# A re-planned order, single-block VectorE rounds and a folded last layer, without zero-weight matmuls

## The chip, the cores and the metric

The kernel runs on one core of a Trainium2 chip. A core has TensorE (PE, matrix products into the accumulation memory PSUM), VectorE (DVE), ScalarE (ACT, activation functions and copies), GpSimd (POOL) and SyncE (SP, here the queue that issues every DMA). The metric is the device time of one execution in microseconds.

## The reference

The input x has 2,048 rows of 512 features. Four layers are applied in turn, A, B, A, B, each to a layer norm of x and each added to x.

```python
def _A_ref(x, wq, wk, wv, wo):          # H = 32 heads, Dh = 16, one shared k and v
    q = (x @ wq).reshape(B, S, H, Dh).transpose(0, 2, 1, 3)
    k = x @ wk; v = x @ wv
    scores = jnp.einsum("bhqd,bkd->bhqk", q, k) * (Dh ** -0.5)
    o = jnp.einsum("bhqk,bkd->bhqd", softmax(scores), v)
    return o.transpose(0, 2, 1, 3).reshape(B, S, H * Dh) @ wo

def _B_ref(x, wqkv, wo):
    q, k, v = split_heads(x @ wqkv)      # 32 heads of 16 each
    phi = lambda t: jnp.where(t > 0, t + 1, jnp.exp(t)) + 1e-6
    pq, pk = phi(q), phi(k)
    kv = jnp.einsum("bhsd,bhse->bhde", pk, v); z = pk.sum(s)
    o = jnp.einsum("bhsd,bhde->bhse", pq, kv) / (pq . z + 1e-6)
    return o.transpose(0, 2, 1, 3).reshape(B, S, D) @ wo

x = x + _A_ref(layernorm(x)); x = x + _B_ref(layernorm(x))
x = x + _A_ref(layernorm(x)); x = x + _B_ref(layernorm(x))
```

Layers 0 and 2 are softmax attention, layers 1 and 3 linear attention.

## The kernel before

x is kept on the chip as 16 tiles of 128 rows (`x_sb`). Everything is issued by a planner: the class `Planner` holds operations with durations (`dur`), latencies (`lat`), priorities (`prio`) and dependencies, runs them through an event queue as the program is built, and writes the order it arrives at as the fixed instruction stream of each engine (`_dispatch1` picks, `emit` writes, with one semaphore wait per producing engine). Nothing is scheduled on the chip itself; a duration that is wrong only makes the fixed order a poor one. PSUM has eight banks: six in two sets of three for score blocks, bank 6 (`ACC`) for the weighted values, bank 7 and what is left over for the rest.

Softmax attention (`run_a`). Queries of a tile lie in four row groups j with two parities, so a layer has 64 segments (`a_segs`) and 2,048 blocks of 128 keys by 512 query columns. TensorE makes scores with 32-row matmuls that lie side by side in the array (L807, three or four in a group), and sums weighted values with 32-column matmuls, four side by side (L861). A block goes one of two ways. `act_stream` gives two or three blocks to one ScalarE exp (L973, 1024 or 1536 wide). One further block may ride along in the same score group and go to VectorE: `dve_take` turns scores into bf16 bit patterns with one add and maximum (L1049), and after each four such blocks `dve_shifts` makes three shifted copies (L1080), whose four versions are summed with weighted values (`VW`). VectorE blocks start only with an exp's score group, when `dve_open` or `dve_split` finds the backlog small enough. ScalarE's stream is in strict order; two sets of banks allow one group of scores to be made while the other is read.

Linear attention (`run_b`). `tile_` makes k and v of a tile, `q_` its q, `phi` their positive map (ScalarE exp at L1205, two VectorE operations). `kv_` sums keys by values over groups of tiles, `den` and `main` form numerator and denominator, divide (L1364, L1420), transpose, project (L575) and add to x (L1448). A tile's work of one layer starts when the layer before has finished that tile, so much of layer 1 lies beside layer 0's attention and much of layer 3 beside layer 2's. Only the last tile's chain and what needs the whole key sum comes after: the handover at 735 to 760 us and the tail after 1508 us.

Zero-weight matmuls. When TensorE has nothing to do the planner lets two functions add work whose stationary operand is zero: `fill` (L906, in attention) and `fill_lin` (L793, elsewhere). `fill` looks at a running count of columns:

```python
n = int(min(512, pl.work(0), (min(nxt) - pl.now) * 2400 if nxt else 512)) // 64 * 64
```

They add zero to a sum or write a bank that is cleared afterwards.

Of the kernel before, what the change touches and what calls it, by code (L numbers as in the profile page):

```python
# [15 lines left out]
P = 128  # L16
# [19 lines left out]
class Planner:  # L36
# [3 lines left out]
    def __init__(self, nc):  # L40
        self.nc = nc
        self.now = 0.0
        self.events = []
        self.seq = 0
        self.ready = {e: [] for e in ENGS}
        self.busy = {e: False for e in ENGS}
        self.until = {e: 0.0 for e in ENGS}
        self.order = {e: [] for e in ENGS}
        self.writer = {}
        self.readers = {}  # L50
        self.flags = {}
        self.flagwait = {}
        self.level = (0.0, 0.0)
        self.due = []
        self.idle = []
        self.mode = None
        self.port = 0.0

# [63 lines left out]
    def _dispatch(self, e):  # L122
        self._dispatch1(e)
        if e == PE and not self.busy[e] and self.idle:
            self.due = [t for t in self.due if t > self.now]
            for f in self.idle:
                f()

    def _dispatch1(self, e):
# [4 lines left out]
        while h:  # L134
# [5 lines left out]
            if o.port and self.port > self.now:  # L140
                held.append(x)
                continue
            if e == PE and STICK and o.mode != "row" and o.mode != self.mode != "row":
# [10 lines left out]
            if e == PE:  # L154
                if self.mode != o.mode:
                    dur += SWITCH
                self.mode = o.mode
# [6 lines left out]
            if o.begun:  # L164
                self.at(self.now, o.begun)
            self.at(self.now + dur, lambda: self._freed(e, o))
# [4 lines left out]
        if held and not self.busy[e] and e != PE:  # L171
# [124 lines left out]
    def emit(self, e, eng):  # L296
        waited = {}
        for o in self.order[e]:
# [7 lines left out]
            for k, d in need.items():  # L306
# [9 lines left out]
class Seg:  # L316
# [11 lines left out]
    def take(self, js, back=False):  # L328
# [12 lines left out]
QK_DUR = 0.225  # L341
PV_DUR = 0.225
QK_LAT = 0.365
SWITCH = 0.105
DH_DUR = 0.22
AH_DUR = 0.28
MCRIT = {0: (), 1: (0, 1), 2: (), 3: ()}
# [11 lines left out]
BLS = 1.4  # L359
BLO = 3.0  # L360
BLT = 4.0
# [6 lines left out]
DENS = {1: [[0], [1], [2], [3], [4], [5], [6], [7], [8, 9], [10, 11], [12, 13], [14, 15]],  # L368
        3: [[0], [1, 2], [3, 4, 5], [6, 7, 8, 9], [10, 11, 12], [13, 14, 15]]}
# [3 lines left out]
RESA = {1: (), 3: ()}  # L373
# [18 lines left out]
def bass_interleave_layers__grouped_kv_mqa__linear_attn_block__prompt_kernel(  # L392
# [42 lines left out]
    eps1 = sb("eps1", [1, H], BF16)  # L435
    warm = sb("warm", [P, 1], FP32)
# [117 lines left out]
    pool_op(lambda e: e.memset(eps1[:], 1e-6), ["eps"], dur=0.1, prio=2.1)  # L554
    pool_op(lambda e: e.memset(mask8[:], 1.0), ["mask8"], dur=0.3, prio=2.3)
# [231 lines left out]
    lin = {"a": False, "next": -1.0}  # L787

    def fill_lin():
        if lin["a"] or pl.busy[PE] or ("x", 3, T - 1) in pl.flags:  # L790
            return
        n = 128
        op({PE: (n / 2300.0, lambda e: e.matmul(ps[0:32, ACC * 512:ACC * 512 + n], lhsT=V0[:], rhs=zz[:], start=True, stop=True))},  # L793
           reads=["zz"], writes=[B_(ACC)], prio=9.0, lat=0.13, mode="col").cols = n

    pl.idle.append(fill_lin)

    def run_a(L):
# [34 lines left out]
        def pv_try():  # L833
# [32 lines left out]
            o = op({PE: (PV_DUR, fn)}, reads=list({x[3] for x in items}) + [("V" if x[5] is None else "VW", x[0]) for x in items], writes=[B_(ACC)], prio=2.0, lat=0.13, mode="col")  # L866
# [15 lines left out]
        def retry():  # L882
            if state.get("next", -1.0) <= pl.now:
                state["next"] = pl.now + 0.1
                pl.at(state["next"], lambda: pl._dispatch(PE))

        def fill():
            if cur["i"] >= len(segs) or state["done"] or not state["on"]:
                return
            sg = segs[cur["i"]]  # L890
            js = [j for j in range(4) if 0 < sg.sent[j] < sg.need[j]]
            spare = [b for b in banks.free if not retire.get(b)] if not banks.wait else []
            nxt = [t for t in pl.due if t > pl.now]
            n = int(min(512, pl.work(0), (min(nxt) - pl.now) * 2400 if nxt else 512)) // 64 * 64
            clear = not sg.submitted and all(o.done for o in pl.ws(B_(ACC)) + pl.readers.get(B_(ACC), []))
            if n >= 128 and not js and not clear and not spare:
                retry()
            if n < 128 or not (js or clear or spare):
                return
            if clear:  # L900
                b, j, st = ACC, 0, True
            elif js:
                b, j, st = ACC, js[-1], False
            else:
                b, j, st = spare[0], 0, True
            o = op({PE: (n / 2400.0, lambda e: e.matmul(ps[32 * j:32 * j + 32, b * 512:b * 512 + n], lhsT=V0[:],  # L906
                                                       rhs=QT[:, sg.t, 0:n], start=st, stop=st))},
                   reads=[("QT", sg.t)], writes=[B_(b)], prio=9.0, lat=0.13, mode="col")
            o.cols = n

        pl.idle.append(fill)

        def act_stream():
# [4 lines left out]
            state["on"] = lin["a"] = True  # L918
            while True:
# [50 lines left out]
                if chunk["blk"] and stale():  # L970
                    dve_close()
                p_ = yield ("acq", pt_pool, 0.0)
                ex = op({AC: (0.05 + 0.4267 * n, lambda e, n=n, s_=s_, p_=p_: e.activation(PT[:, p_, 0:n * 512], ps[:, s_ * 512:(s_ + n) * 512], ACTF.Exp, scale=EXPSC, bias=EXPBIAS))},  # L973
                        writes=bk + [("PT", p_)], prio=1.0, lat=0.17)
                ex.begun = lambda n=n: pl.due.append(pl.now + 0.05 + 0.4267 * n + 0.17)
                pl.give_after(sets, s_, [ex] if split is None else [ex, p1])
                pv_post(ex, [(sg, kt, j, PT[:, p_, i * 512:(i + 1) * 512], ("PT", p_)) for i, (sg, kt, j) in enumerate(group)], [n, [], pt_pool, p_])
            state["done"] = True
            pv_kick()
# [64 lines left out]
        def dve_take(extra, own):  # L1044
# [4 lines left out]
            o = op({DV: (0.60, lambda e: e.tensor_scalar(out=dst.bitcast(I16), in0=bank(b), scalar1=VB, scalar2=VLO, op0=ALU.add, op1=ALU.max))},  # L1049
# [7 lines left out]
            return o  # L1057

# [7 lines left out]
        def dve_shifts(blk, f_, hold):  # L1066
# [3 lines left out]
            for w in range(1, NSH):  # L1070
# [8 lines left out]
                en, du = (PO, n / 1165.0 + 0.25) if pool else (DV, n / 3840.0 + 0.066)  # L1079
# [117 lines left out]
    ph_pool = Pool_(range(NPH))  # L1197

    def run_b(L):
# [3 lines left out]
        def phi(b, dst, key, pr, n=D, join=None, after=()):  # L1203
            i = yield ("acq", ph_pool, pr)
            op({AC: (0.07 + n / 1200.0, lambda e: e.activation(phE[:, i, 0:n], bank(b, n), ACTF.Exp))}, reads=[B_(b)], writes=[("phE", i)], prio=min(pr, 0.9))  # L1205
# [22 lines left out]
        def crit_v(t, sl, pr):  # L1228
# [5 lines left out]
            for h in range(2):  # L1234
                src, dst = bank(bs[h], 256).rearrange("p (h d) -> p h d", d=DH), va_v[:, sl, 16 * h:16 * h + 16, 0:DH]
                c = op({AC: (AH_DUR, lambda e, dst=dst, src=src: e.copy(dst, src))}, writes=[B_(bs[h]), ("va", sl)], prio=pr, join=l)
# [4 lines left out]
        def tile_(t):  # L1241
# [19 lines left out]
            src, dst = bank(b).rearrange("p (h d) -> p h d", d=DH), va_v[:, sl, :, 0:DH]  # L1261
            if t >= CRIT:
# [7 lines left out]
        def q_(t):  # L1270
            pr = base(t) + 0.01 * t + 0.2
            yield ("flag", ("xnT", L, t))
            yield from until(("xnT", t))
            b = yield ("acq", banks, pr)
            mm4(bank(b), lambda g, k: wqkv[:, k, g * P:(g + 1) * P], lambda k: xnT[:, k, t * P:(t + 1) * P], [("xnT", t), "wqkv"], b, pr)
            yield from phi(b, QT[:, t, :], ("QT", t), pr)
            pl.flag(("bq", L, t))

# [175 lines left out]
        for t in range(T):  # L1454
            pl.process(tile_(t))
            pl.process(q_(t))
            pl.process(main(t))
        for ts in DENS[L]:
            pl.process(den(ts))
        for gi, ts in enumerate(KVG):  # L1460
            pl.process(kv_(gi, ts))
# [50 lines left out]
```

## Time and profile before

| | |
|---|---|
| median of 3 runs | 1555.51 us (1555.47 to 1560.37) |
| profiled execution, its own time | 1556.79 us |
| its span | 1555.1 us |
| PE, DVE, ACT busy share | 94%, 93%, 95% |
| first and last attention exp | 13.6 and 1508.0 us, with none from 736.2 to 759.5 |
| zero-weight matmuls, busy | 131.0 us (L906), 16.1 us (L793) |

A group's line gives source line, engine, operation, written and read tensors, shapes and count; then busy time and mean duration of one; then idle time of the engine ahead of them and what ended it. Matmul durations include the way through the array, so side-by-side matmuls overlap and a busy PE need not be at its peak. PEclk is the clock granted to TensorE, as a share of full speed.

### The profile page before, as it was taken

What the parts mean: (1) busy time and instruction counts of PE and PEld (TensorE: products, weight loads), DVE (VectorE), ACT (ScalarE), POOL (GpSimd) and SP (SyncE); (2) the same over time, 40 slices, a digit from 0 to 9 for tenths busy, and PEclk for the clock granted to TensorE, in tenths of its full rate; (3) what the DMA queues carried; (4) which work ended last, traced back from release to release, by engine and by line L of the source; (5) the groups of instructions that cost most, each with busy time, mean ns of one, the idle gap of its engine ahead of it and who ended that gap; (6) DMA issues with size and microseconds to landing.
All of it is one profiled execution on the core that took longest, in us unless ns stands there. A gap on an engine that the chain in (4) does not pass through costs nothing.

```text
span 1555.1 us, 36056 instructions
## 1 busy us (share of the span) xinstructions
PE 1458.7 (94%) x14602; PEld 535.4 (34%) x14713; DVE 1448.3 (93%) x2707; ACT 1476.8 (95%) x1500; POOL 68.8 (4%) x122
## 2 busy tenths in 40 slices
PE   8998999999999999999999989999999999999999
PEld 4322332333333333333644323323333333333345
DVE  7999999999999999998676799999999999999977
ACT  8999999999999999999699999899999999999982
POOL 4000000000000000000111000000000000000000
PEclk9999999999999999999999999999999999999998
DMA  5100010000000000000000000000000000000001
GB/s 132 47 2 1 8 22 5 8 8 5 8 8 8 5 8 5 1 1 1 2 1 1 1 1 15 15 8 8 6 9 5 8 8 8 5 5 2 1 2 55
DMA packets 40435, 17.55 MB, mean 11 GB/s; under 512 B 34128, under 2 KB 39760, under 8 KB 40272
## 3 DMA queue, kind: packets, MB, share of 16 engines
q1 hardware_dynamic: 40272, 15.25, 4.2%
q8 instruction: 118, 1.93, 0.5%
q14 instruction: 45, 0.37, 0.1%
HBM read 5.28 MB, written 2.10 MB: 5 GB/s over the span
## 4 chain that ended last, share of the span: by engine, by line
PE 32%; issue 23%; DVE 23%; ACT 20%; POOL 1%; DMA 0%; SPq 0%; ACTq 0%; POOLq 0%; DVEq 0%
ACT PT L973 19%; DVE FB L1049 11%; PE ps L861 11%; PE ps L807 9%; DVE FB L1080 6%; PE ps L575 4%; PE ps L906 2%; PE ps L732 2%; PE ps L1122 1%; POOL rs L655 1%; DVE st L651 1%; DVE sacc L1103 1%; PE ps L793 1%; ACT phE L1205 1%; DVE xn L658 1%
## 5 line engine op out<-in xcount | busy, mean ns | idle before, releaser
L973 ACT ACTIVATE PT<-ps 128x1024 bf16<-128x1024 f32 (+1 forms) x1361 | 1424.5, 1180 | 19.9 <-PE ps L861 13.4
L1049 DVE TENSOR_SCALAR FB<-ps 128x512 int16<-128x512 f32 x1017 | 675.0, 686 | 23.5 <-PE ps L807 20.7
L807 PE MATMUL ps<-QT,KM 32*128 32x512 bf16 x4096 | 533.4, 384 | 46.8 <-ACT PT L973 27.9
L861 PE MATMUL ps<-FB,VW 128*32 128x512 bf16 x4068 | 530.4, 385 | 19.5 <-ACT PT L973 9.5
L861 PE MATMUL ps<-PT,V 128*32 128x512 bf16 x3079 | 513.0, 386 | 9.7 <-ACT PT L973 5.6
L1080 DVE TENSOR_SCALAR FB<-FB 128x2048 int16<-128x2048 int16 (+1 forms) x765 | 503.0, 683 | 0.9
L807 PEld LDWEIGHTS ps<-QT,KM 32*128 32x128 bf16 x4096 | 139.8, 91 | 445.3 <-ACT PT L973 203.8
L861 PEld LDWEIGHTS ps<-FB,VW 128*32 128x32 bf16 x4068 | 133.4, 94 | 219.5 <-issue 113.0
L861 PEld LDWEIGHTS ps<-PT,V 128*32 128x32 bf16 x3079 | 125.9, 94 | 111.8 <-issue 56.1
L906 PE MATMUL ps<-QT,V 128*32 128x512 bf16 (+6 forms) x568 | 131.0, 315 | 0.9 <-DVE FB L1049 0.9
L655 POOL TENSOR_TENSOR rs<-ve,mhalf 128x1 f32<-128x1 f32 x64 | 51.7, 811 | 1398.9 <-DVE ve L653 1386.0
L575 PE MATMUL ps<-wqkv,xnT 128*128 128x512 bf16 (+1 forms) x211 | 65.1, 368 | 3.9 <-issue 2.9
L906 PEld LDWEIGHTS ps<-QT,V 128*32 128x32 bf16 x568 | 44.1, 95 | 59.6 <-issue 39.3
L1103 DVE COPY sacc<-ps 128x512 f32<-128x512 f32 x64 | 43.8, 684 | 7.8 <-PE ps L861 7.6
L1205 ACT ACTIVATE phE<-ps 128x512 bf16<-128x512 f32 (+1 forms) x66 | 41.3, 625 | 6.6 <-PE ps L732 4.7
L1122 PE MATMUL ps<-identF,sacc 128*128 128x128 f32 x256 | 45.9, 291 | 1.5 <-DVE sacc L1103 0.8
L732 PE MATMUL ps<-xnT,wqkv 128*128 128x128 bf16 x512 | 44.3, 221 | 0.0
L651 DVE BATCH_NORM_STATS2 st<-x_sb 128x6 f32<-128x512 bf16 x60 | 40.8, 683 | 2.6 <-DMA x_sb<-in_A_x_dram 2.3
L1105 DVE TENSOR_TENSOR sacc<-sacc,ps 128x512 f32<-128x512 f32 x56 | 38.2, 682 | 2.4 <-PE ps L861 2.1
L732 PE MATMUL ps<-xnT,wq 128*128 128x128 bf16 x480 | 38.6, 224 | 0.0
L575 PEld LDWEIGHTS ps<-wqkv,xnT 128*128 128x128 bf16 x272 | 21.8, 97 | 44.9 <-issue 34.2
L732 PEld LDWEIGHTS ps<-xnT,wqkv 128*128 128x128 bf16 x512 | 29.1, 98 | 22.8 <-issue 19.4
(115 smaller groups left out, 671.1 us busy)
## 6 DMA issues: line engine op xcount, KB each, us to landing
out_dram<-x_sb SPq DMA_DIRECT2D x16, 128.0 KB, 1.7
x_sb<-in_A_x_dram SPq DMA_DIRECT2D x3, 512.0 KB, 6.1
wqkv<-in_B_wqkv_dram SPq DMA_DIRECT2D x1, 1536.0 KB, 7.5
xnT<-xn SPq DMA_TRANSPOSE x36, 2.4
x_sb<-in_A_x_dram SPq DMA_DIRECT2D x4, 128.0 KB, 2.2
wq<-in_A_wq_dram SPq DMA_DIRECT2D x1, 512.0 KB, 4.2
wo<-in_A_wo_dram SPq DMA_DIRECT2D x1, 512.0 KB, 4.1
wo<-in_B_wo_dram SPq DMA_DIRECT2D x1, 512.0 KB, 8.5
```

What stands on the lines that cost most here:

```text
L575: return e.matmul(dst, lhsT=l, rhs=r, start=(k == 0), stop=(k == len(pairs) - 1))
L655: op({PO: (0.55, lambda e: e.tensor_tensor(out=rs[:, t:t + 1], in0=ve[:, t:t + 1], in1=mhalf[:], op=ALU.pow))}, reads=[("ve", t), "mhalf"] ...
L732: ins = e.matmul(dst[:, g * P:(g + 1) * P], lhsT=lhs(g, k), rhs=rhs(k), start=(k == 0), stop=(k == FT - 1))
L807: return e.matmul(bank(b), lhsT=KM[r, sg.par, kt * P:(kt + 1) * P], rhs=QT[r, sg.t, :], start=True, stop=True)
L861: ins = e.matmul(ps[32 * j:32 * j + 32, ACC * 512:(ACC + 1) * 512], lhsT=V[:, kt, :] if w is None else VW[:, kt, w, :], rhs=ap, start=(k = ...
L906: o = op({PE: (n / 2400.0, lambda e: e.matmul(ps[32 * j:32 * j + 32, b * 512:b * 512 + n], lhsT=V0[:], rhs=QT[:, sg.t, 0:n], start=st, sto ...
L973: ex = op({AC: (0.05 + 0.4267 * n, lambda e, n=n, s_=s_, p_=p_: e.activation(PT[:, p_, 0:n * 512], ps[:, s_ * 512:(s_ + n) * 512], ACTF.Ex ...
L1049: o = op({DV: (0.60, lambda e: e.tensor_scalar(out=dst.bitcast(I16), in0=bank(b), scalar1=VB, scalar2=VLO, op0=ALU.add, op1=ALU.max))}, wr ...
L1080: o = op({en: (du, lambda e, w=w, g_=g_: e.tensor_scalar(out=FB[:, g_, 0:n].bitcast(I16), in0=FB[:, f_, 0:n].bitcast(I16), scalar1=float(w ...
L1103: o = op({DV: (0.6, lambda e, src=src: e.tensor_copy(src, bank(ACC)))}, writes=[B_(ACC), key], prio=0.0, lat=0.15)
L1122: o = op({PE: (0.12, lambda e, c=c: e.transpose(ps[:, b * 512 + c * P:b * 512 + (c + 1) * P], src[:, c * P:(c + 1) * P], identF[:]))}, rea ...
L1205: op({AC: (0.07 + n / 1200.0, lambda e: e.activation(phE[:, i, 0:n], bank(b, n), ACTF.Exp))}, reads=[B_(b)], writes=[("phE", i)], prio=min ...
```

## The change

- `fill` and `fill_lin` are gone; what they read stays in memory, unused.
- `alone`: when VectorE's ready list is empty or its backlog under `DXB`, a single score matmul is issued for one VectorE block, in a free bank, without an exp.
- Planner: `soon` holds back a VectorE or ScalarE operation outside attention when a more urgent one will be ready before it would end; TensorE's cost of changing its mode is reduced by idle time; waits of one instruction are written in the order in which they are expected to end. Durations, latencies and backlog limits are set anew.
- Layer 1: q of tiles 4 to 13 starts after the last exp of layer 0 (`QLATE`); at most three q are under way.
- Layer 3 is folded. Keys by values are summed transposed (`kvt`) and multiplied with the output weights once (`mix`, giving 512 by 512). Per tile, `den3` forms every feature's denominator with four matmuls against a block-diagonal z, takes its reciprocal on ScalarE as exp(-ln(d + 1e-6)), and multiplies q with it on VectorE (tiles 4, 7 and 10 on GpSimd); `main3` is then four matmuls and the add to x (tiles 3, 7 and 11 add x on TensorE and copy on ScalarE).

```diff
-        pl.idle.append(fill)
...
+        def alone():
+            if state["done"] or not USE_DVE or ("K", L, KGATE) not in pl.flags or not banks.free or banks.wait or pl.backlog(DV) > DXB:
+                return
+            hit = dve_hit(set())
+            if hit is None:
+                return
+            x = hit + (banks.free.pop(0),)
+            qo = op({PE: (QK_DUR, lambda e: qk_mm(e, x[3], x[0], x[1], x[2]))}, reads=qk_reads(x[0], [x[1]]), writes=[B_(x[3])], prio=0.1, lat=QK_LAT - QK_DUR, mode="row")
+            qo.cols = 128
+            dve_take(x, True)
...
-QK_DUR = 0.225
-PV_DUR = 0.225
-QK_LAT = 0.365
-SWITCH = 0.105
+QK_DUR = 0.22
+PV_DUR = 0.222
+QK_LAT = 0.438
+SWITCH = 0.107
+ROWIN = 0.07
+PV_LAT = 0.215
+EX_LAT = 0.21
...
+QLATE = {1: range(4, 14), 3: ()}
...
-BLS = 1.4
-BLO = 3.0
-BLT = 4.0
+BLS = 1.2
+BLO = 5.0
+DXB = 2.0
+BLT = 3.0
...
         def q_(t):
...
+            if t in QLATE[L]:
+                yield ("flag", ("exps", L - 1))
...
+        def mix(g):
+            pr = 1.45 + 0.001 * g
+            b = yield ("acq", banks, pr)
+            mm(bank(b), [(kvT[:, g, :], wo2[:, g, :])], ["kvT", "wo2"], b, pr, 0.216)
...
+        def den3(t):
...
+            op({PE: (0.23, fn)}, reads=[("QT", t), "Zbd"], writes=[B_(b)], prio=pr, lat=0.2).cols = 512
+            af = [("FB", f_, i % 2 * 2), ("FB", f_, i % 2 * 2 + 1)]
+            o = op({AC: (0.5, lambda e: e.activation(rd, bank(b), ACTF.Ln, bias=epsc[:]))}, reads=["epsc"], writes=[B_(b), ("rd", i)], prio=pr, after=af)
+            pl.give_after(banks, b, [o])
+            op({AC: (0.5, lambda e: e.activation(rd, rd, ACTF.Exp, scale=-1.0))}, writes=[("rd", i)], prio=pr)
+            qn = FB[:, 1 + t // 4, t % 4 * 512:t % 4 * 512 + 512]
+            o = op({(PO if t in PQ else DV): (PQD if t in PQ else 0.6, lambda e: e.tensor_tensor(out=qn, in0=rd, in1=QT[:, t, :], op=ALU.mult))}, reads=[("rd", i), ("QT", t)],
+                   writes=[("qn", t)], prio=pr, after=[("FB", 1 + t // 4, t % 4)])
...
+        def main3(t):
...
+                mm(bank(b), pairs, keys, b, pr, 0.86 + SW[L] / 2)
+                o = op({DV: (0.6, lambda e: e.tensor_tensor(out=x_sb[:, t, :], in0=x_sb[:, t, :], in1=bank(b), op=ALU.add))},
+                       writes=[B_(b), ("x", t)], prio=pr)
```

## The prediction

> **What bounds the kernel now.** I read the page first, then the groups of instructions with their shapes kept apart, then busy time by stretch, then the timeline of TensorE. The page's slices come first:
>
> ```profile
> span 1555.1 us, 36056 instructions
> PE   8998999999999999999999989999999999999999
> DVE  7999999999999999998676799999999999999977
> ACT  8999999999999999999699999899999999999982
> PEclk9999999999999999999999999999999999999998
> ```
>
> Three engines are near full in the two attention layers, ScalarE most evenly. The stretches show who has room, and where:
>
> ```profile
> 13.00:720.00 707.00, 666.20 (x6663) 226.28 (x6710) 690.33 (x1265) 700.55 (x701) 28.28 (x40) 1.00 0.05 12
> 735.00:760.00 25.00, 23.86 (x304) 18.36 (x302) 14.04 (x46) 9.83 (x25) 2.05 (x4) 1.00 0.01 1
> 760.00:885.00 125.00, 117.80 (x1168) 51.38 (x1177) 89.10 (x193) 123.91 (x114) 13.57 (x29) 1.00 0.01 1
> 885.00:1500.00 615.00, 578.13 (x5744) 195.50 (x5789) 598.49 (x1080) 602.56 (x605) 16.34 (x15) 1.00 0.04 7
> 1508.00:1519.00 11.00, 11.00 (x138) 9.05 (x136) 6.67 (x21) 3.96 (x10) 0.55 (x1) 1.00 0.01 1
> 1519.00:1555.00 36.00, 32.45 (x289) 20.39 (x291) 27.00 (x46) 7.34 (x13) 0.00 (x0) 0.86 0.18 59
> ```
>
> The columns are length, then busy time of PE, PE loads, DVE, ACT and POOL, then the clock. ScalarE is idle 6.5 us of 707, 1.1 of 125 and 12.4 of 615: it sets the pace of attention. It rests 15.2 us in the handover at 735 to 760, and in the tail after 1519 it does only 7.3 us of 36. VectorE has 36 us of room at 760 to 885. Now the groups that the change touches:
>
> ```profile
> L973 ACT ACTIVATE PT<-ps 128x1024 bf16<-128x1024 f32 x1004 | 972.9, 1067 | 16.2 <-PE ps L861 11.8 <-PE ps L807 3.3
> L973 ACT ACTIVATE PT<-ps 128x1536 bf16<-128x1536 f32 x357 | 511.3, 1497 | 3.7 <-PE ps L807 1.8 <-PE ps L861 1.6
> L1205 ACT ACTIVATE phE<-ps 128x512 bf16<-128x512 f32 x62 | 39.7, 641 | 4.8 <-PE ps L732 4.7
> L562 ACT ACT_TABLE_LOAD x1 | 1.3, 1283 | 0.8 <-PEq L1497 0.8
> L906 PE MATMUL ps<-QT,V 128*32 128x512 bf16 (+6 forms) x568 | 131.0, 315 | 0.9 <-DVE FB L1049 0.9
> L793 PE MATMUL ps<-zz,V 128*32 128x128 bf16 x198 | 16.1, 228 | 0.0
> ```
>
> The last two are the zero-weight matmuls; nothing waits for them. Back-to-back ScalarE instructions overlap: start to start in the trace most exps are 0.904 us apart (1024 wide) and 1.331 us (1536), and the 512-wide ones 0.477.
>
> What the zero-weight matmuls may do shows in the clock, which leaves 1.0 at two places, 24.02 to 27.43 us and 1522.47 to 1532.7:
>
> ```profile
> 20.61:24.02 3.41, 3.01 (x42) 1.58 (x39) 3.41 (x13) 3.41 (x4) 1.99 (x5) 1.00 0.39 79
> 24.02:27.43 3.41, 3.08 (x16) 1.10 (x16) 2.48 (x10) 3.21 (x4) 1.78 (x4) 0.50 0.28 46
> 573.57:576.98 3.41, 2.33 (x22) 0.79 (x23) 3.41 (x7) 3.41 (x5) 0.00 (x0) 1.00 0.02 5
> 1519.06:1522.47 3.41, 3.41 (x60) 2.81 (x58) 3.36 (x8) 0.60 (x1) 0.00 (x0) 1.00 0.00 0
> ```
>
> PE's busy time does not tell these stretches apart; the columns streamed do. Four 512-column matmuls side by side show 0.40 us and eight 0.61, so a group takes 0.21. In multiples of that, matmuls streamed 44% of 20.61 to 24.02 and 19% of 1519.06 to 1522.47, and the clock halved after each; 43% of 573.57 to 576.98 did not halve it. The border is near 44%.
>
> **The change part by part.** The sum is made against the profiled execution's 1556.8 us (span 1555.1); the median of the runs is 1555.5, 1.3 below.
>
> *Exps.* In the built order of the new program ScalarE has 947 exps of 1024, 387 of 1536 and one of 512. At the distances above: -57 x 0.904 + 30 x 1.331 + 0.48 = -11.1 us. A few more copies of 0.47 us fall to ScalarE: +2.
>
> *Late q.* Ten tiles of the first linear layer compute q only after the first attention's last exp. Their ScalarE exps, 10 x 0.477 = 4.8 us, leave the full stretch and can lie in the 15.2 idle us of the handover: -5. Their 16 matmuls (1.07 us a tile) stand on TensorE behind the handover's own chain, which is hidden as long as that chain has the pauses that 7.4 us of zero-weight matmuls fill today. Tiles 4 to 13 of the second attention wait for these q; it begins with tiles 0 to 3.
>
> *Other waits.* Durations and sorted waits are re-planned. Bounds: 0, and all 19.9 us of idle before the exps. The VectorE rounds issued alone answer only part of what those rows name, so I take a third: -6. Attention together: -20, with ends -9 and -34 (-11 + 2, alone or with -5 and -20).
>
> *VectorE rounds.* 1,040 evictions instead of 1,017 and 783 shifts instead of 765, 0.60 us start to start: 24.7 us more. The cover is the 36 us at 760 to 885 and 8 us that late q frees (10 x 0.80); without it up to 24.7 would come back. Zero.
>
> *TensorE.* 147 us of zero-weight matmuls go. The program now holds 3,505 groups of score and value matmuls instead of 3,422, 70 of them a lone score matmul: 83 x 0.22 = 18 us more, in the freed time. POOL gets three multiplies in the tail (128x128 took 0.415 us, so an estimate of 1.7 each) beside 2.4 us per tile on ScalarE. SyncE's queue has the same transposes and stores in almost the same order: zero.
>
> *The clock in attention.* Counted again without the zero-weight columns, 28 of some 420 stretches of 3.41 us fall below 44%, against 1 with them. Laying the new order's matmuls beside its exps at the distances above I count about 20 (24 for the old order by the same method, so it counts a little low). The price of one: below, 0.3 us, what ScalarE lost in and after 24.02 to 27.43 (0.20 + 0.12), where no VectorE round hung on TensorE; above, half the stretch, 1.7. Attention asks TensorE for some 65% of its columns, so a halved stretch leaves about a quarter undone; between the ends I take 0.7: +14, with ends 0 (no fall) and 34.
>
> The row at 20.61 has only 0.40 us of idle PE and still precedes a fall. The Trainium skill, "TensorE: Matmul & The Clock Gate", section "HAM oscillation", puts the danger at idle gaps of TensorE above some 3.4 us; by that rule nothing in attention would fall, and the sum would lose the 14.
>
> *The clock in the tail's chain.* In 1512.23 to 1515.65 the real columns are 35% without L793, whose 37 matmuls run there for 2.2 us while the chain waits. The next matmuls (16 in 1.91 us) would run at half: +3, ends 0 and 6.
>
> *The folded last layer.* Now the tail needs 36.4 us from the last kv matmul to the end. New, per tile: four small matmuls, Ln and Exp on ScalarE, one multiply, four matmuls, one add. The built order has Ln and Exp in groups of two tiles with an activation table load ahead of each group, 18 loads. A pair of tiles: 2 x 1.283 + 2 x (0.48 + 0.64) = 4.81 us. VectorE needs 2 x 2 x 0.60 = 2.4 for it and TensorE about 2.1 (8 x 0.22 + 8 x 0.05), so ScalarE sets the tail. From there: masked z 0.7, first scores 0.4, Ln 0.6, load and Exp 1.8, two copies 1.0, seven pairs 33.7, a lone tile 3.8, three copies 1.4, then multiply, matmuls, add and 2.4 us of store: 5.3. That is 48.7 instead of 36.4; with a half-clocked end 0.7 more: +13. Ends: +10 (all at the short distance), and +36 if every load costs twice its row, since the one load seen had an idle engine before it. Should loads cost nothing here, -10.
>
> The load's row has no drain beside it. The Trainium skill, "ScalarE: Activation LUTs", section "What ACT_TABLE_LOAD costs", gives about 2.66 us for a switch, a drain of 1.38 included; 18 x 1.38 would add an estimated 25 us, 1591 in all.
>
> **Sum.** 1556.8 - 20 + 14 + 3 + 13 = 1566.8; against the median 1565.5, so 1566.
>
> **The rivals.**
> 1. *The clock holds* (faster). Place: attention and the tail's chain. For it: 573.57 stayed at 1.0 with 43%, and two falls are all the evidence for a border. Against: the fall at 24.02 with 44%. Both clock terms vanish: 1556.8 - 20 + 13 - 1.3 = 1548.5. It decides when the two clock terms together are under 2.3 us, some three cold stretches. The Trainium skill's rule, named under the clock in attention, would make this the outcome.
> 2. *Cold stretches at full price*: 20 x 1.7 = 34 instead of 14: 1586. For it: nearly all idle before the exps (15.1 of 16.2 us of the 1024-wide ones) already waits for TensorE. Against: the small loss at 24.02.
> 3. *A switch costs twice the load*: +23: 1589. For it: the only load row is before any work. Against: the activation after it followed at once. The Trainium skill's figure, named above, points here.
> 4. *The loads cost nothing* (the fold does what it can): -23: 1543. Against: the 1.283 us row. The Trainium skill, "ScalarE: Activation LUTs", section "Table sets", names a set that holds both functions; the built order loads between them all the same.
>
> **How the numbers follow.** Chances: forecast 0.40 (own range 1555 to 1577), rival 1 0.28, rival 2 0.15, rival 3 0.12, rival 4 0.05. Runs of this kernel tell 0.3% (4.7 us) from no change. Faster: three quarters of rival 1, rival 4 and a sliver of the forecast: 0.27; same: the rest of rival 1 and the forecast's low edge: 0.09; slower 0.64. Range 1541 to 1595: it cuts off about 0.07 below (rival 4 and the best of 1) and 0.10 above.
>
> **What would show it.** Right: clock rows of 0.50 scattered through 60 to 1490; exps ending about 6 us earlier than 1508 net; ScalarE above 90% busy in the tail with 18 loads of 1.28; a tail near 49 us. Wrong: a clock of 1.00 throughout attention, loads with idle time behind them, or a last exp after 1515.

## The result and the profile after

The changed kernel takes 1605.38 us (median of 4 executions, 1603.94 to 1606.78) against 1557.94 us of the kernel before beside it (1555.47 to 1561.19): 1.0313 times as long, interval 1.0297 to 1.0329. The direction was forecast, the size was not: 1605 lies beyond the range's upper end of 1595. The profiled execution took 1606.78 us, its span is 1604.9.

Lines of the page of the changed kernel, the same ones as shown of the kernel before:

```profile
span 1604.9 us, 34443 instructions
PE   7998998988888989888999888999988988899965
DVE  7999999999999999997776999999999999999943
ACT  7999999999999999997899998999999999999967
PEclk9989999999998998899999999999999999998977
```

The clock row has dips all along, and TensorE shows tenths of 8 where it had 9. At the right end VectorE and TensorE run down while ScalarE goes on. The stretches of the changed kernel (length, then busy time of PE, PE loads, DVE, ACT and POOL, the clock, DMA share and GB/s) are cut at its own first and last exps:

```profile
15.00:730.00 715.00, 638.53 (x6276) 206.95 (x6324) 688.45 (x1256) 696.20 (x672) 25.58 (x40) 0.96 0.05 12
745.00:773.50 28.50, 27.23 (x345) 21.62 (x345) 21.07 (x64) 13.28 (x34) 2.56 (x5) 0.94 0.01 2
773.50:900.00 126.50, 115.32 (x1142) 51.31 (x1150) 92.45 (x200) 120.80 (x115) 13.39 (x29) 0.95 0.01 1
900.00:1500.00 600.00, 535.28 (x5345) 175.48 (x5392) 583.94 (x1051) 582.38 (x578) 11.92 (x14) 0.97 0.03 7
1534.68:1550.00 15.32, 10.86 (x82) 6.47 (x76) 5.72 (x16) 3.35 (x9) 0.55 (x1) 0.80 0.00 1
1550.00:1604.90 54.90, 30.57 (x132) 13.00 (x135) 20.04 (x31) 45.38 (x56) 3.46 (x3) 0.72 0.12 39
```

ScalarE's idle time in the three attention stretches is now 18.8, 5.7 and 17.6 us, and the clock is 0.95 to 0.97 there. The groups say what ScalarE waits for:

```profile
L965 ACT ACTIVATE PT<-ps 128x1024 bf16<-128x1024 f32 x947 | 921.0, 1048 | 23.5 <-PE ps L828 15.2 <-PE ps L882 5.2 <-PE ps L762 0.2
L965 ACT ACTIVATE PT<-ps 128x1536 bf16<-128x1536 f32 x387 | 550.9, 1471 | 16.2 <-PE ps L828 11.2 <-PE ps L882 3.4
L1384 ACT ACT_TABLE_LOAD x9 | 11.5, 1283 | 0.2
L1386 ACT ACT_TABLE_LOAD x9 | 11.5, 1283 | 0.2
L1384 ACT ACTIVATE FB<-ps,epsc 128x512 f32<-128x512 f32 x16 | 10.2, 684 | 0.1
L1386 ACT ACTIVATE FB<-FB 128x512 f32<-128x512 f32 x16 | 9.3, 622 | 0.1
```

Idle before the exps was 19.9 us (16.2 + 3.7), two thirds of it for value matmuls; it is 39.7 now, 26.4 of it for score matmuls (L828). A wait that moves to the matmuls straight ahead of the exp is what a slower TensorE looks like. A fall is one or more stretches of 3.41 us in a row at 0.50. Within the span there are 25 falls, 140 us in all, against two falls and 13.7 us before. Here is one, the stretch ahead of it first:

```profile
489.61:493.02 3.41, 1.83 (x19) 0.59 (x19) 3.26 (x8) 3.41 (x4) 0.86 (x1) 1.00 0.03 7
493.00:496.41 3.41, 3.41 (x20) 0.62 (x17) 2.85 (x5) 2.86 (x4) 0.00 (x0) 0.50 0.16 33
```

In the first, matmuls streamed in 31% of the time; in the second TensorE is busy throughout at half speed and ScalarE stands still for 0.55 of 3.41 us.

Where the 49.9 us of span went, from the last attention exp's end (1507.98 us before, 1534.68 after): 26.7 us up to it, 23.2 behind it in what is called the tail below (47.1 us before, 70.3 after).

### The profile page after: what moved, and what is told of

It reads as the page before. It is cut to its first block, busy times and chain, and to the rows that moved or that the text cites. A ratio compares the mean times of both kernels' runs of the same rounds, so it can differ in the third digit from the quotient of the medians.

```text
span 1604.9 us, 34443 instructions
## 1 busy us (share of the span) xinstructions
PE 1407.3 (88%) x13836; PEld 495.2 (31%) x13943; DVE 1462.4 (91%) x2728; ACT 1516.9 (95%) x1521; POOL 66.2 (4%) x126
## 4 chain that ended last, share of the span: by engine, by line
PE 35%; DVE 31%; ACT 27%; issue 6%; DMA 0%; SPq 0%; POOL 0%; ACTq 0%; DVEq 0%; POOLq 0%
ACT PT L965 24%; PE ps L882 15%; DVE FB L1044 14%; PE ps L828 11%; DVE FB L1086 9%; PE ps L605 3%; PE ps L762 2%; PE ps L1128 2%; DVE sacc L1111 1%; DVE sacc L1109 1%; ACT phE L1213 1%; DVE st L681 1%; ACT L1386 1%; ACT L1384 1%; ACT FB L1384 1%
## 5 line engine op out<-in xcount | busy, mean ns | idle before, releaser
L965 ACT ACTIVATE PT<-ps 128x1024 bf16<-128x1024 f32 (+1 forms) x1335 | 1421.7, 1170 | 39.6 <-PE ps L828 26.4
L1044 DVE TENSOR_SCALAR FB<-ps 128x512 int16<-128x512 f32 x1040 | 687.0, 684 | 32.2 <-PE ps L828 28.6
L828 PE MATMUL ps<-QT,KM 32*128 32x512 bf16 x4096 | 550.0, 394 | 72.5 <-ACT PT L965 41.8
L882 PE MATMUL ps<-FB,VW 128*32 128x512 bf16 x4160 | 562.0, 397 | 39.6 <-ACT PT L965 27.8
L882 PE MATMUL ps<-PT,V 128*32 128x512 bf16 x3056 | 528.9, 396 | 30.7 <-ACT PT L965 29.3
L1086 DVE TENSOR_SCALAR FB<-FB 128x2048 int16<-128x2048 int16 (+1 forms) x783 | 510.8, 679 | 0.8
L828 PEld LDWEIGHTS ps<-QT,KM 32*128 32x128 bf16 x4096 | 141.6, 91 | 481.0 <-ACT PT L965 155.6
L882 PEld LDWEIGHTS ps<-FB,VW 128*32 128x32 bf16 x4160 | 139.4, 95 | 260.7 <-issue 124.5
L685 POOL TENSOR_TENSOR rs<-ve,mhalf 128x1 f32<-128x1 f32 x64 | 45.5, 714 | 1436.2 <-DVE ve L683 1426.7
L1213 ACT ACTIVATE phE<-ps 128x512 bf16<-128x512 f32 (+1 forms) x66 | 39.9, 606 | 12.1 <-PE ps L762 7.2
L1128 PEld LDWEIGHTS ps<-identF,sacc 128*128 128x128 f32 x256 | 28.3, 145 | 22.8 <-issue 9.1
L605 PE MATMUL ps<-FB 128*128 128x512 bf16 x62 | 23.5, 531 | 13.0 <-DVE FB L1388 7.0
L1388 DVE TENSOR_TENSOR FB<-FB,QT 128x512 bf16<-128x512 f32 x13 | 9.4, 731 | 27.2 <-ACT FB L1386 27.2
```

Of the source, the lines that this page charges most:

```text
L605: return e.matmul(dst, lhsT=l, rhs=r, start=(k == 0), stop=(k == len(pairs) - 1))
L828: return e.matmul(bank(b), lhsT=KM[r, sg.par, kt * P:(kt + 1) * P], rhs=QT[r, sg.t, :], start=True, stop=True)
L882: ins = e.matmul(ps[32 * j:32 * j + 32, ACC * 512:(ACC + 1) * 512], lhsT=V[:, kt, :] if w is None else VW[:, kt, w, :], rhs=ap, start=(k = ...
L965: ex = op({AC: (0.051 + 0.4267 * n, lambda e, n=n, s_=s_, p_=p_: e.activation(PT[:, p_, 0:n * 512], ps[:, s_ * 512:(s_ + n) * 512], ACTF.E ...
L1044: o = op({DV: (0.602, lambda e: e.tensor_scalar(out=dst.bitcast(I16), in0=bank(b), scalar1=VB, scalar2=VLO, op0=ALU.add, op1=ALU.max))}, w ...
L1086: o = op({en: (du, lambda e, w=w, g_=g_: e.tensor_scalar(out=FB[:, g_, 0:n].bitcast(I16), in0=FB[:, f_, 0:n].bitcast(I16), scalar1=float(w ...
```

## The experiments

Theories at the start. Clock theory: the missing fills let the clock fall, and that costs some 35 to 43 us; the folded layer costs some 16 to 23 through its loads; the re-planned order costs nothing. Rival: the new order is slow of itself. All later kernels are compared with the kernel before on the same chip, whose median was between 1555.4 and 1557.0 us in these comparisons.

### Each part put back, and taken away alone

`e1_fills_back` restores both functions in the changed kernel:

```diff
+    pl.idle.append(fill_lin)
...
+        pl.idle.append(fill)
```

> The changed kernel with the zero-weight matmuls put back (both kinds, in attention and in the linear layers), all else as changed. Clock theory: what the missing fills cost is the clock, 33 us of late exps over the 31 stretches at .50 in attention and some 7 us in the linear layers and the tail, and the rest of the change is worth little either way; so the clock row stays at 1.00 through attention and the time falls from 1605 by 35 to 43 us, to 1562 to 1570. Rival (the new order is slow of itself, and the clock falls are a by-product of waits): the clock comes back and the time stays above 1590.

1575.71 us, ratio 1.013 (1.0113 to 1.0146): 29.7 us less, where 35 to 43 were forecast. The clock in attention came back but for one fall of 6.8 us; falls stayed in the tail. The planner takes the fills into its plan, so the built order is not quite that of the changed kernel: 966 exps of 1024 and 376 of 1536 instead of 947 and 387.

`e2_before_no_fills` takes the same two lines out of the kernel before.

> The kernel before, without the zero-weight matmuls and with nothing else changed. Clock theory: 25 to 35 falls in attention, and 30 to 45 us more than before: 1588 to 1603. Rival (the new order is to blame): few falls, since the old order was tuned round a full clock, and under 10 us more: below 1568. Third possibility, the planner's dispatches change where the fills go (a matmul need no longer wait for a fill in front of it): faster than before by up to 5 us with the clock at 1.00.

1594.22 us, 1.0242 (1.022 to 1.0264): 38.8 us more, with 17 falls and 122.9 us at .50 in attention (17.1 of them at 24 us, where the kernel before has 3.4). In the old order too the wait moves to the score matmuls (L806 here), as the exps' groups of this run show:

```profile
L971 ACT ACTIVATE PT<-ps 128x1024 bf16<-128x1024 f32 x993 | 968.0, 1068 | 30.6 <-PE ps L806 15.1 <-PE ps L860 12.8
L971 ACT ACTIVATE PT<-ps 128x1536 bf16<-128x1536 f32 x363 | 522.0, 1499 | 18.6 <-PE ps L806 15.3 <-PE ps L860 2.5
```

The rival, that the old order keeps its clock, is out. The fills are worth more to it than to the new one.

`e3_old_last_layer` gives the changed kernel the old form of layer 3, still without fills; `e4_fills_old_last_layer` has both the fills and the old layer.

```diff
+FOLD = False
...
-RESA = {1: (), 3: (3, 7, 11)}
+RESA = {1: (), 3: ()}
...
-            pl.process((main3 if L == 3 else main)(t))
+            pl.process((main3 if FOLD and L == 3 else main)(t))
...
-            pl.process((kvt if L == 3 else kv_)(gi, ts))
+            pl.process((kvt if FOLD and L == 3 else kv_)(gi, ts))
```

> The changed kernel with the last linear layer in its old form (denominators by 8-column matmuls and a reciprocal on VectorE, no Ln, no table loads) and still no fills. Fold theory: the tail loses the 18 loads of 1.28 us and half of its ScalarE work; it comes from 70 us back to 48 to 55 us (old form at a partly halved clock), so 1584 to 1592. Rival (the tail is long because TensorE is at half clock there, and the form of the layer is no matter): the tail stays over 62 us and the time over 1597.

> The changed kernel with the fills put back and the last linear layer in its old form: what is left of the change is the re-planned order with the single-block VectorE rounds. If the costs of the two parts add up, 1605 less 35 to 43 for the clock less 16 to 23 for the tail: 1540 to 1554, faster than before by up to 18 us. If the new order yields nothing (the warm part of attention after has the same 45 us of late exps as before's 47), only the 12 us fewer ScalarE busy time is left: about 1546. If the new order is slow of itself: over 1560.

e3 took 1582.48 us (1.0173, 1.015 to 1.0195), its tail 47.8 us, both just under what was forecast. e4 took 1557.18 us, ratio 1.0011 (1.0001 to 1.0021). So the medians form a chain: before 1555.5; re-planned order and lone rounds (the single-block VectorE rounds) +1.7; no fills +25.3; folded layer +22.9; together the changed kernel's 1605.4. e4 missed its forecast: of the re-plan's gain nothing arrives, with the clock at 1.00.

### The loads

One table holds ln and exp; `e5_one_table` loads it once, ahead of ScalarE's stream, in e1. Every other instruction stays in its place.

```diff
-        block.scalar(lambda e: pl.emit(AC, e))
+        block.scalar(lambda e: (e.preload_act_table_set("natural_log_exp_and_others"), pl.emit(AC, e)))
```

> The changed kernel with the fills back, and one table that holds both exp and ln loaded once at ScalarE's start, so that the 18 loads of the last layer go and every other instruction stays where it is. Load theory (ScalarE sets the tail): 18 loads of 1.295 us leave ScalarE's line, less what TensorE and VectorE then take as the next bound, 15 to 23 us off the run with the fills back (1575.7): 1553 to 1561. Rival (TensorE at half clock is the tail's second bound, right behind): at most 8 us off, 1568 or more.

1549.57 us, 0.9963 (0.995 to 0.9976): 26.1 us less than e1, more than the 15 to 23 forecast. The tail went from 64.9 to 38.2 us. First ScalarE's timeline of the changed kernel's tail (start, length, instruction), one pair of tiles:

```profile
1555.17 1.28 ACT L1384 ACT_TABLE_LOAD   x1
1556.46 1.27 ACT L1384 ACTIVATE FB<-ps,epsc 128x512 f32<-128x512 f32 x2
1557.75 1.28 ACT L1386 ACT_TABLE_LOAD   x1
1559.04 1.15 ACT L1386 ACTIVATE FB<-FB 128x512 f32<-128x512 f32 x2
1560.21 1.28 ACT L1384 ACT_TABLE_LOAD   x1
```

and the same work in e5:

```profile
1523.86 1.28 ACT L1424 ACTIVATE FB<-ps,epsc 128x512 f32<-128x512 f32 x2
1525.01 1.16 ACT L1426 ACTIVATE FB<-FB 128x512 f32<-128x512 f32 x2
1526.05 1.28 ACT L1424 ACTIVATE FB<-ps,epsc 128x512 f32<-128x512 f32 x2
```

A pair takes 1560.21 - 1555.17 = 5.04 us with loads and 2.19 without. A switch costs 1.43 us (2.85 by two): the load's 1.28 and 0.14 of overlap that the instructions on both sides lose. The Trainium skill, "ScalarE: Activation LUTs", section "What ACT_TABLE_LOAD costs", has 1283 ns for the load, as here, and a drain of about 1.38 us besides, which this trace does not show: the next activation starts 1.29 us after the load does.

`e11_one_table_no_fills` is the changed kernel with the one table and nothing else.

> The changed kernel with the one table and no fills: the 18 loads go, the clock stays as it falls. If loads and clock add up: 1605 less 23 to 26, 1579 to 1583, and the difference to the run with fills and one table (1549.6) is the fills' 30 us. Rival (in the tail the loads hide TensorE at half clock, which sets the end once they are gone): 1587 to 1597, with TensorE's waits in the tail.

1580.5 us (1.0143, 1.0119 to 1.0168). Loads and fills add up: the loads are 24.9 us here and 26.1 with fills, the fills 30.9 us here and 29.7 with loads.

### How many fills

`e8_fewer_fills` sets the old kernel's aim to 4000 columns a stretch, `e12_more_fills` that of e5 to 6000:

```diff
-WORK = 5000
+WORK = 4000
```

> The kernel before with the fill matmuls aimed at 4000 streamed columns per 3.41 us instead of 5000. Border theory (the clock falls after a stretch with under about 44% of 8192 columns, some 3600): the clock stays at 1.00, there are some 200 to 400 fewer fills, and the time is the same or a little less, 1549 to 1556. Rival (the border lies between 4000 and 5000, or the planner's count is too rough for a margin of 400): 3 to 12 falls of the clock in attention and 1558 to 1572.

> The changed kernel with fills and one table (1549.6), with the fills aimed at 6000 columns per 3.41 us in place of 5000. The executions of one kernel differ by 0.35 us for each us at .50, so with no fall at all it would be 1548.4. Clock theory: 1547 to 1549.5, and a spread under 2 us. Rival (a fill delays the matmul behind it, and past 5000 there is nothing left to win): 1551 to 1556.

e8 took 1565.66 us (1.0063, 1.0048 to 1.0078), with three falls, 20.5 us, in attention: the rival's case. The planner's count is too rough for 4000. e12 took 1549.94 us (0.9964, 0.9953 to 0.9975), level with e5. Six of its eleven executions had no fall at all and took 1549.4 to 1549.9; five still fell, up to 1555.4, so neither the time nor the spread shrank. Past 5000 there is nothing left to win, and more fills cost about a microsecond.

Where the border lies can be counted over seven profiles (before, after, e1 to e4, e8). Their stretches of 3.41 us, without the start and the tail, sorted by the share of time in which any matmul streamed (0.213 us for 512 columns, about the distance of groups in the prediction):

| share streamed | stretches | followed by one at .50 |
|---|---|---|
| under .40 | 67 | 57 |
| .40 to .42 | 26 | 14 |
| .42 to .47 | 88 | 16 |
| .47 to .52 | 99 | 2 |
| .52 and more | 2751 | 0 |

In before the lowest stretch is at .43, in after 35 are under .42. A stretch at .50 is followed by another in 33 of 92 cases, one at full speed in 56 of 2939.

### Where the attention's gain went

Taking back one part of the re-plan at a time, first in e4:

`e6_no_lone_rounds` (`pl.hungry = []` in place of `[alone]`) and `e7_no_late_q` (`QLATE` with no tile).

> The re-planned order with fills and the old last layer (1557.2), without the single-block VectorE rounds. That run had 6.8 us less exps than the kernel before, and 7 us more waits among them. Theory (the lone score matmuls, a change of TensorE's mode each, delay the groups that ScalarE waits for, and give back what VectorE takes over): exps' work grows by 6 to 9 us and the waits shrink as much, 1554 to 1560. Rival A (the lone rounds pay, and the planner's other constants cost it): 1561 to 1567. Rival B (they only cost): under 1553.

> The re-planned order with fills and the old last layer (1557.2), with the query tiles 4 to 13 of the first linear layer no longer held back until the exps of the attention before are done. The prediction had them at a gain of 5 us, so 1562 without. Theory after the first runs: they moved 3.7 us of ScalarE work out of the first attention and 2.2 us into the gap between the two exp stretches, so a gain of 1 to 3 us: 1558 to 1561. Rival (the gap pays for all of it): 1554 to 1557.

e6: 1559.52 us (1.0018, 1.0008 to 1.0028), within the bounds of the first theory, but not for its reason: the exps hardly grew (1376.8 us against 1376.1) and the waits did not shrink (57.8 us against e4's 56.6). e7: 1561.62 us (1.0036, 1.002 to 1.0052), just above its forecast and 4.4 us slower than e4. Its executions spent more time at .50; at the same time at .50 (by the 0.35 us per us counted in the last section) the late q are worth some 3.5 us.

Then in e5 (1549.57 us), the limits and the planner's costs as before:

```diff
-BLS = 1.2
-BLO = 5.0
-BLT = 3.0
+BLS = 1.4
+BLO = 3.0
+BLT = 4.0
```

> The changed kernel with fills and one table (1549.6), with the three limits on VectorE's planned backlog as in the kernel before (1.4, 3.0 and 4.0 us in place of 1.2, 5.0 and 3.0). The new order has 7 us less exps and 7 us more waits among them than the old. If the limits are what trades one for the other without a gain: the same within 2 us, 1547.5 to 1551.5. If the limits alone make the waits: 1542 to 1547. If they are what gains: 1552 to 1557.

> The changed kernel with fills and one table (1549.6), with the planner's durations and latencies of the attention's matmuls and exps as in the kernel before (the latency of a score group 0.365 in place of 0.438, of a value group 0.13 in place of 0.215, of an exp 0.17 in place of 0.21). If the new costs describe the chip better, as an order planned with them should show: slower, 1552 to 1557. If they make the planner hold work back that could have run, and so make the 7 us more waits: 1542 to 1547. If a planner's cost of a few hundredths is no matter: 1548 to 1551.5.

`e9_old_thresholds`: 1563.9 us (1.0052, 1.0033 to 1.0071), 14 us slower, beyond all that was expected. `e10_old_durations` (the constants from `QK_DUR` to `EX_LAT`): 1554.5 us (0.9992, 0.998 to 1.0003), 4.9 us slower. Each of four parts costs 2 to 14 us when it is taken back, and all together yield nothing against the old order. So the same parts were put into the old order:

> The kernel before with nothing of the change but the folded last layer, and one table. If the re-planned order as a whole yields nothing (1557.2 against 1555.5), this is level with the changed kernel with fills and one table (1549.6) or a little ahead: 1546 to 1550.5. Rival (the re-plan yields some 5 us or more that the pairing with the old last layer hid): 1553 or more.

> The kernel before (1555.5 to 1557) with only the three limits on VectorE's planned backlog as changed (1.2, 5.0, 3.0 us). In the new order, taking them back cost 14 us. If they pay by themselves, this is faster: 1542 to 1550, and another part of the re-plan costs 20 us. If limits and order only fit together, taking over one alone is slower: 1559 to 1572. If it is neither, 1553 to 1558.

> The run before last in this list (the old order with the folded layer and one table) with only the late query tiles added. In the new order they were worth 4.4 us (3.3 at the same clock). If a moved transformation of query tiles pays by itself, 2 to 5 us under that run. If ScalarE's time only moves from the attention to the gap behind it: within 1.5 us.

> The kernel before with the new limits and the single-block VectorE rounds, nothing else of the change. The lone rounds were worth 2.5 us in the new order. If limits and lone rounds are a pair (one fills the gaps that the other leaves on VectorE), this is faster than the new limits alone by 3 us or more, and than the kernel before: under 1552. If the planner's other changes are needed for both: 1558 to 1570.

- `e13_old_order_one_table` (before, plus `kvt`, `mix`, `den3`, `main3` and the one table): 1550.02 us (0.9955, 0.9944 to 0.9967), level with e5. The whole re-plan nets nothing, with either last layer.
- `e14_before_new_limits`: 1552.99 us (0.9984, 0.9972 to 0.9997), 3.6 us faster than before, some 2.3 at the same time at .50. `e16_before_limits_lone`: 1550.3 us (0.9955, 0.9939 to 0.997), 6.3 us faster, 6.1 at the same time at .50. The two parts pay on their own.
- `e15_old_order_late_q` (e13 with the late q): 1554.91 us (0.9991, 0.9981 to 1.0001), 4.9 us slower than e13 and some 3.6 at the same time at .50, where up to 5 us faster was thought possible.

The windows of e13 and e15 show where the gain went. First the time from the start of the first attention's last exp to the first exp of the second, then the 80 us after it, and a later stretch, e13:

```profile
736.92:761.13 24.21, 23.19 (x292) 17.80 (x290) 14.03 (x46) 9.21 (x24) 2.04 (x4) 1.00 0.01 1
761.13:841.13 80.00, 76.81 (x757) 33.38 (x757) 55.79 (x127) 79.20 (x72) 9.77 (x21) 1.00 0.01 2
986.00:1061.00 75.00, 72.95 (x691) 22.53 (x688) 74.54 (x135) 74.11 (x78) 2.13 (x2) 1.00 0.05 8
```

and e15:

```profile
729.31:761.27 31.96, 31.41 (x433) 25.49 (x427) 23.23 (x69) 15.76 (x35) 2.44 (x5) 1.00 0.01 2
761.27:841.27 80.00, 77.79 (x706) 33.16 (x709) 53.33 (x123) 74.08 (x66) 9.33 (x20) 0.91 0.01 1
986.00:1061.00 75.00, 71.54 (x678) 23.06 (x670) 73.95 (x137) 67.03 (x72) 2.63 (x3) 1.00 0.04 9
```

and the first 80 us of the second attention in e17 (below), which has no late q:

```profile
760.56:840.56 80.00, 76.14 (x702) 33.12 (x708) 53.49 (x123) 74.08 (x66) 9.39 (x20) 0.91 0.01 1
```

The first attention's last exp starts 7.6 us earlier (736.92 to 729.31), the handover from there is 7.75 us longer, with ScalarE busy for 6.6 us more and VectorE for 9.2. So the second attention starts where it did, and nothing is gained. What e15 loses comes later: its last exp ends at 1518.3 us, e13's at 1510.1. In the first 80 us ScalarE is idle for 5.9 us instead of 0.8, but that is a fall of the clock (0.91) which e17 shows at the same place, with the same 74.08 us, without late q. The other large loss is at 986 to 1061 us, at full clock: 8.0 us idle instead of 0.9. Why the late q should cause that is not shown.

The chain of waits in e15's handover begins with 3.7 us of matmuls for the moved tiles (L736). Then (start, length, engine, what) it goes through their positive maps on VectorE (`QT`, L1214), and the statistics of a layer norm that the chain needs (`st`, L636) come between them:

```profile
738.01 0.69 DVE QT L1214
...
739.14 0.69 DVE QT L1214
...
740.03 0.34 DVE st L636
740.37 0.59 DVE QT L1214
740.96 0.35 DVE st L636
```

That left the re-plan's costs, and the late q with the planner's rule for the linear layers:

> The old order with the new limits and lone rounds (6.3 us under the kernel before) and the folded last layer with one table (6.5 us under it). If the two add up, as fills and loads did: 1542 to 1546, the fastest kernel of this study. If the attention's gain depends on the plan of the last layer (the planner's order of the second attention moves with it): 1546 to 1551.

> The same with the planner's new durations, latencies and its rule for a change of TensorE's mode. With the whole re-plan it was 1549.6. If these costs are what takes the gain back: 1548 to 1552, and the late query tiles and the rule for the linear layers are worth nothing more. If they pay (taking the durations and latencies back in the new order cost 4.9 us): under 1543. If neither, they and the late tiles depend on each other: within 2 us of the run without.

`e17_limits_lone_fold` (e13 with limits and lone rounds): 1548.15 us (0.9959, 0.9946 to 0.9973); the gains of e16 and e13 do not add up. One reason shows in the profiles: e16's tail, in the old form, has no fall and takes 43.1 us instead of 47.1, so the fold wins only 3.2 us of tail there (39.9 in e17) and not the 8.7 of e13 (38.4). `e18_limits_lone_new_costs` (e17 with the new durations, latencies and mode-change rule): 1542.44 us (0.9918, 0.9905 to 0.9932), the fastest of the study and faster than both kernels:

```profile
span 1543.1 us, 36080 instructions
ACT  8999999999999999999699999999999999999996
PEclk9999999999999999999999999999999999999999
```

e18 differs from e5 in that it has neither the late q nor the planner's new treatment of the linear layers (`soon`, at most three q, sorted waits, phi's priorities); a few planned durations differ besides, by up to 0.002 us. Together these cost 7.1 us, 5.7 at the same time at .50. The exps of both and their waits (start to start, less the undisturbed distance of each form, over both attentions; the split between other work and waits is good to 1 or 2 us; the gap runs from start to start):

| us | before | e5 | e18 |
|---|---|---|---|
| exps at undisturbed distance | 1382.8 | 1374.2 | 1373.0 |
| other ScalarE work among them | 38.6 | 36.7 | 43.0 |
| waits among them | 49.7 | 59.3 | 52.0 |
| gap between the attentions | 24.4 | 26.5 | 24.2 |
| end of the last exp | 1507.98 | 1509.27 | 1504.34 |

The idle time that the profile shows ahead of the exps tells the same, first e5, then e18:

```profile
L1005 ACT ACTIVATE PT<-ps 128x1024 bf16<-128x1024 f32 x966 | 942.7, 1056 | 13.2 <-PE ps L891 7.8 <-PE ps L837 2.8
L1005 ACT ACTIVATE PT<-ps 128x1536 bf16<-128x1536 f32 x376 | 539.3, 1490 | 10.0 <-PE ps L891 6.5 <-PE ps L837 2.7
L982 ACT ACTIVATE PT<-ps 128x1024 bf16<-128x1024 f32 x1000 | 973.9, 1059 | 12.3 <-PE ps L815 5.7 <-PE ps L869 4.5
L982 ACT ACTIVATE PT<-ps 128x1536 bf16<-128x1536 f32 x352 | 507.3, 1495 | 6.8 <-PE ps L815 3.8 <-PE ps L869 2.4
```

It is 23.2 us in e5 and 19.1 in e18, against 19.9 before. Most of the rest of the waits is overlap lost: an exp starts before the one ahead of it has ended, but later than the undisturbed distance allows. How the 7 us divide between late q and that rule was not tried: in e4's order the late q gained 4.4, in e13's they cost 4.9 (about 3.5 each at the same time at .50). By the same count e7, without late q, still has about 60 us of waits, as e4 and e5 have 57 and 59; so late q alone did not make them in that order, and the rule is the likelier part.

## Why the prediction was wrong, step by step

By the two traces and e1 between them, in us of span:

| step | forecast | measured | from |
|---|---|---|---|
| attention, order and exps | -20 | +2.6 | last exp 1507.98 before, 1510.55 in e1 |
| clock in attention | +14 | +24.1 | last exp 1510.55 in e1, 1534.68 after |
| clock in the tail's chain | +3 | +5.4 | tail 64.9 in e1, 70.3 after |
| folded last layer | +13 | +17.8 | tail 47.1 before, 64.9 in e1 |
| sum | +10 | +49.9 | spans: +49.9 |

*Exps.* Right: by their counts the exps need 1371.7 us instead of 1382.8, -11.1 as worked out. In the order that the fills give (e1, e5) it is -8.6. ScalarE did get less to do.

*Other waits.* The step that failed, and the largest miss of all. It took -6 from bounds of 0 and -19.9, as if waits could only shrink, and it knew them only as idle time of ScalarE, where 19.9 us show; start to start they were 49.7. With the fills back they grew by 9.6 us (the table's 49.7 to 59.3; the idle rows alone by 3.3), about as much as the exps gave. In e5 the attention's sum is then -8.6 for exps, -1.9 for other ScalarE work, +2.1 for the handover and +9.6 for waits: +1.2, where -20 was forecast. Why the waits grew is not shown. Fewer exps do not do it by themselves: e18 has fewer still and 52.0 us of waits. It lacks the late q and the new rule for the linear layers, and more points to the rule.

*Late q.* The size was nearly right in the new order with the fills, where e7 puts it at 4.4 us (3.5 at the same time at .50) against 5. The cover was not there, though: "hidden as long as that chain has the pauses" did not hold. The handover grew by 2.1 us in e4 and e5, by 4.1 in the changed kernel, where the clock falls in it, and by 7.75 in e15, which ate the whole gain. Idle ScalarE time there was not free room: in e15 the moved tiles' matmuls open the handover's chain, and each q also brings two VectorE operations to it. The prediction named TensorE's queue as what the moved tiles pass, and left VectorE's out.

*VectorE rounds* and *TensorE*, both put at zero: nothing shows that they cost anything; without lone rounds e4 was 2.3 us slower.

*The clock in attention.* The mechanism was right, the number of stretches was not, and the price was low. There are 21 falls against "about 20" stretches; but in a third of the cases (33 of 92) the stretch after one at .50 is at .50 too, and 21 falls are 31 stretches. At 24.1 us for 31 that is 0.78 us each, where 0.7 was taken. By the starts of the exps in and right after cold stretches it is 33.2 us, 1.07 each, of which some 6 are what the rest of the attention loses to waits in as much time. From one execution to another of one kernel it is 1.2 (last section). A reason for the lower figure may be that the fills themselves cost time: carried on at 0.35 us per us to no time at .50, an estimate over 90 to 140 us, the four kernels without fills would be 5 to 9 us below the same ones with them.

*The clock in the tail's chain.* Within its ends of 0 and 6, and a matter of the form: the folded layer loses 5.2 to 5.4 us (43.4 in e11 against 38.2 in e5), the old one nothing (47.8 in e3, 47.9 in e4, with 10.2 us at .50 in both). The 16 matmuls named took 3.24 us instead of 1.91.

*The folded layer.* The loads were counted at their own length; a pair came to 5.04 us instead of 4.81. And the tail's TensorE falls to .50 while it waits for ScalarE: 20 us in e1, under 1 in e5. All in all the loads are 26.7 us (64.9 - 38.2) and not 23.1. Without them the tail is 9.7 us shorter than the old layer's with fills (38.2 against e4's 47.9): the end of -10 that was given for it. Part of that is the clock: old tails with less time at .50 took 44.8 us (e7) and 43.1 (e16).

*Rivals.* The clock did not hold (1); cold stretches cost about half to two thirds of the full price (2); a switch costs 1.43 us and not twice the load's 1.28 (3); the loads were not free (4), though one line makes them so. The Trainium skill's rule, "TensorE: Matmul & The Clock Gate", section "HAM oscillation", named beside the first rival, speaks of idle gaps over some 3.4 us; here, in the changed kernel's attention, falls followed stretches with 23% to 46% of streaming, and in none of these was TensorE idle for more than 1.4 us at once.

No rival joined two errors. The range came from single cases; all four terms missed to the same side.

## What to carry to other kernels

Work that only keeps TensorE streaming looks like waste in a profile and pays through the clock: count streamed time per clock stretch before it is removed, and expect falls to last longer than one stretch. When an order is planned anew, let the bound of "other waits" reach to the loss side too, by as much as the gain: here they grew by that much. Measure them from start to start, since the idle rows show less than half. Before a table switch is accepted, ask for one table that holds both functions; and take the parts of a re-plan one by one, because parts that pay 2 to 14 us each in one order can net nothing together.

## What the runs showed of the hardware

- The executions of one program differ by how long its clock stood at .50, and by little else. For 23 executions of the kernel before (span and mean clock give 3 to 25 us at .50, the time 1553.7 to 1561.0) the slope is 0.35 us per us at .50, 1.2 us for a stretch; for the 12 of e7 it is 0.35 as well (3.1 us: 1557.7 and 1558.7; 34.5 us: 1569.3). Comparing two orders within a few us means comparing them at the same time at .50.
- The clock's border is a band: between .40 and .47 of streamed time a stretch may or may not be followed by a fall (30 of 114).
- An activation next to a table load loses the overlap with its neighbour: two Ln and two Exp take 1.29 and 1.17 us up to the load behind them, 1.15 and 1.04 us up to the next activation where there is none.
